# A fused FFT filter and mixture of experts: result tiles of 128 rows, earlier routing, fewer expert steps per filter piece, two result banks

## The chip, the cores and the metric

The kernel runs on one core of one Trainium2 chip. The metric is the device time of one execution in microseconds (us); the runs shown are the kernel before, three times: 1031.1, 1027.1 and 1033.96 us, median 1031.1.

The engines have the names of the profile: PE multiplies matrices (PEld is its weight load), DVE and ACT work on vectors, POOL here mostly issues DMAs with row indices, SP issues the other DMAs. Each engine works through its own queue in order.

## The reference

`x` is [8, 2496, 256]: 8 batches of 2496 tokens with 256 channels. Each batch is filtered along its tokens in the frequency domain, and each filtered token then goes through one of eight experts:

```
y      = irfft(rfft(x, axis=1) * (filt_r + 1j * filt_i), n=2496, axis=1)
logits = y @ w_gate + modality_bias[modality_id]        # [19968, 8]
e      = argmax(logits);  p = softmax(logits)[e]
out    = p * (relu(y @ w1[e]) @ w2[e])                  # w1 [8,256,1024], w2 [8,1024,256]
```

## The kernel before

**The filter** is a transform in two factors, 2496 = 48 x 52, with matrices that are made at the start. A batch goes through three stages, each in pieces of two columns; between the stages the data is turned by writing it to DRAM and reading it back in another order.
- Stage 1 (`stage1`, 13 pieces): two products with `w1m` (L363), ACT evicts them to `t1` (L366), SP writes `b1_d` (L369) after every second piece.
- Stage 2 (`stage2`, 12 pieces, the second half of a piece one step later): SP loads `t2` (L379); two products with `w2m` (L382); ACT evicts to `xf` (L394); DVE multiplies by the filter (L396, L397); four products with `a1m`, `a2m` (L389, L390); ACT evicts `z` (L403); SP writes `b2_d`.
- Stage 3 (`stage3`, 13 pieces, also one step apart): SP loads `t4`; two products with `wbm` (L433) give two result tiles of 96 tokens each; ACT and DVE in turn evict them to `yo` (L451, L453); four transposes (L441), DVE's copy `yT` (L443), four products with the gate weights (L446), and DVE adds them to the logits `lg` (L456). So a batch is 26 result tiles of 96 rows.

All these products, and the routing's, take their PSUM tiles from one pool of four banks, `fpsum`. The tile of the transposes holds the gate products as well.

**Routing.** `route` (DVE, one pair of small PE products with `psO`, L478 and the line behind it) finds each token's expert and its slot in `bins_d`, a DRAM table with a region for each expert. `table` (DVE) then makes the list of full blocks that a batch adds. `scatter` (L501, POOL, an indirect DMA) writes one result tile of 96 rows, token number and gate weight beside the data, to these slots; a batch has 26.

**The experts.** A block is 256 tokens of one expert; there are 85 (`KR` = 1, 10, 10, 10, 9, 10, 10, 25 by batch). SP loads it (`xs`, L575), five buffers. `turn` reads the expert's number into a register of PE (L584, `values_load`) and of DVE, copies the expert's first weights to `w1` (DVE, L588), copies the token numbers and gate weights to `meta` (DVE, L594, three buffers), transposes the block on PE (L598) and evicts it to `xT` (L599). Then follow four steps. Step q is `up` for the q-th quarter of this block's hidden units (four products, L609, then ACT's `hT`, L614) and `down` for the same quarter of the block before (four products, L622, which pick the second weights by PE's register). `turn` of the next block stands behind the second step. The result collects in one PSUM bank, `ops`, that opens with the first `down`; after the last, DVE evicts it in two halves times the gate weight to `osb` (L629, two buffers), and POOL writes each half to the rows of `out` that `meta` names (L632, an indirect DMA).

**The order** is that of the loops in the program; a scheduler keeps the order on each engine except where `behind(what, n)` puts an instruction behind a mark. Iteration `i` runs piece k = 0 to 13 of stage 1 for batch `i`, stage 2 for batch `i-1`, stage 3 for batch `i-2` and the scatters (two a piece) for batch `i-3`, then three expert steps (`STEPS`). After the pieces come `route` and `table` of batch `i-2`; blocks of batch `i-3` are opened for the experts then, at the end of its scatters. After iteration 11 the rest of the blocks run alone.

Of the kernel before, what the change touches and what calls it, by code (L numbers as in the profile page):

```python
# [28 lines left out]
def kernel(  # L29
# [32 lines left out]

    BLK = 256
# [48 lines left out]
    STEPS = 3  # L112
# [187 lines left out]
    keep = const_pool.tile([KA, E, NTT], F32)  # L300
# [40 lines left out]
    pp = ctx.enter_context(tc.tile_pool(name="fpsum", bufs=4, space=bass.MemoryType.PSUM))  # L341
# [7 lines left out]
    NP = NTT // EV  # L349
    st = [dict() for _ in range(B)]  # L350
# [57 lines left out]
    def stage3(g, k):  # L408

        t = k * EV  # L410
        if k == 0:
            yw = yp.tile([KA, NTT, RW], I32, tag="yo", name="yo")
            st[g]["yw"] = yw
            nc.gpsimd.iota(yw[:, :, DW:DW + 1], pattern=[[1, NTT], [1, 1]], base=g * S, channel_multiplier=NTT)
            mid_raw = sp.tile([KA, NTT, 2], I32, tag="midr")
            nc.sync.dma_start(mid_raw, mid32[g * S:(g + 1) * S].rearrange("(p t) two -> p t two", t=NTT))
            midf = sp.tile([KA, NTT], F32, tag="midf")
            nc.vector.tensor_copy(midf, mid_raw[:, :, 0])
            lg = sp.tile([KA, NTT, E], F32, tag="lg", bufs=2)
            st[g]["lg"] = lg  # L420
            nc.vector.tensor_mul(lg, midf[:, :, None].to_broadcast([KA, NTT, E]),
                                 biasd[:KA, None, :].to_broadcast([KA, NTT, E]))
            nc.vector.tensor_add(lg, lg, bias0[:KA, None, :].to_broadcast([KA, NTT, E]))
        yo = st[g]["yw"].bitcast(BF16)
        if k < NP:
            c, t0, t1 = chunk_of(t)
            if t == t0:
                src = b2_d[g].rearrange("s (jr t) c -> (s jr) t c", jr=4)
                st[g]["t4"] = bp.tile([KA, TCM, D], BF16, tag="t24", name="t4")
                nc.sync.dma_start(st[g]["t4"][:, 0:t1 - t0, :], src[:, t0:t1, :])  # L430
            ps = pp.tile([P, EV, D], F32, tag="ps")
            for i in range(EV):
                nc.tensor.matmul(ps[:KA, i, :], lhsT=wbm, rhs=st[g]["t4"][:, t - t0 + i, :], start=True, stop=True)  # L433
        if k > 0:
            tb = t - EV
# [317 lines left out]
```

## Time and profile before

| what | value |
|---|---|
| profiled execution, its time | 1031.97 us |
| its span in the profile | 1030.2 us |
| median of the three runs shown | 1031.1 us |
| mean granted clock of PE | 0.868 |
| busy, PE / DVE / POOL / ACT | 662.1 / 424.8 / 409.0 / 387.0 us |
| expert products, up / down | 222.2 / 227.6 us busy, 1360 each |
| scatters / output writes on POOL | 193.7 us for 208 / 166.8 us for 170 |
| routing products of the eight batches start at | 170.5, 244.5, 317.9, 416.7, 517.2, 612.8, 704.7, 796.3 us |

The times are of one execution, taken by the hardware profiler; all terms below are set against its 1031.97 us. A row of the groups reads: line, engine, operation, tiles, count, busy time, mean of one, idle time of the engine before them and what ended it. In a row of waits, "DVE meta L594 <- DMA out_dram" means that DVE's instruction of L594 had nothing to do until that DMA was seen to be done; the numbers are total, times and longest. In a row of the timeline the same stands in brackets behind the instruction. "remote" and "another core or an unknown queue" are waits whose releaser the profile does not know; this program has one core. "issue" is idle time without any wait. The granted clock reads 1.00 up to about 245 us of this trace, although products start 0.21 us apart there; from then on 0.50 and 1.00 take turns.

### The profile page before, as it was taken

The numbers are of one execution on the slowest core, as the hardware profiler recorded it, in microseconds if no ns is written. First come the engines' busy times: TensorE is split into PE (matmuls) and PEld (weight loads), VectorE is DVE, ScalarE is ACT, GpSimd is POOL, SyncE is SP. The second block draws the span as 40 slices with busy tenths as digits, with TensorE's granted clock in tenths as the row PEclk, the third lists the DMA queues.
The fourth block names the chain that finished last, engine by engine and source line by source line (L and its number), as shares of the span: only waits on it lengthen the run. The fifth ranks groups of instructions, "written<-read, shape, count | busy, mean of one in ns | idle before, by whom it ended". The sixth has DMA issues, their size and how long they took to land.

```text
span 1030.2 us, 16235 instructions
## 1 busy us (share of the span) xinstructions
PE 662.1 (64%) x4966; PEld 526.6 (51%) x4966; DVE 424.8 (41%) x1305; ACT 387.0 (38%) x697; POOL 409.0 (40%) x468
## 2 busy tenths in 40 slices
PE   0316377266645777687677776774777567768776
PEld 0205266255434666566565555563555445656554
DVE  8803145135325344633454463445335322333332
ACT  1115255143433455344444443441333233434333
POOL 6022201712442355435535543544355455333333
PEclk9999999999655898589979986896868787999999
DMA  9299965335436445534553344324111422212210
GB/s 146 36 207 208 219 147 127 91 91 129 108 87 140 115 120 116 129 99 126 123 146 92 96 120 111 91 62 113 58 57 54 118 68 78 73 62 67 68 42 2
DMA packets 95179, 106.66 MB, mean 104 GB/s; under 512 B 13226, under 2 KB 77520, under 8 KB 94994
## 3 DMA queue, kind: packets, MB, share of 16 engines
q0 software_dynamic: 32544, 52.04, 23.0%
q1 hardware_dynamic: 62554, 53.59, 20.1%
q8 instruction: 45, 0.74, 0.3%
q14 instruction: 36, 0.29, 0.1%
HBM read 74.27 MB, written 54.31 MB: 125 GB/s over the span
## 4 chain that ended last, share of the span: by engine, by line
PE 30%; issue 22%; DMA 13%; DVE 12%; another core or an unknown queue 10%; POOL 7%; ACT 4%; DVEq 1%; POOLq 0%; ACTq 0%; SPq 0%
PE hps L609 7%; PE ops L622 7%; DMA t<-b_d 5%; POOL out_dram L632 4%; DMA b_d<-t 4%; POOL bins_d L501 3%; DMA b_d<-z 2%; PE ps L433 2%; PE pz L389 2%; PE lt L446 2%; PE ps L363 2%; PE pz L390 2%; PE ps L382 2%; DVE osb L629 2%
## 5 line engine op out<-in xcount | busy, mean ns | idle before, releaser
L614 ACT ACTIVATE hT<-hps 128x512 f16<-128x512 f32 x340 | 197.0, 597 | 305.0 <-PE hps L609 164.3
L632 POOL DMA_INDIRECT out_dram<-osb,meta x170 | 166.8, 981 | 308.8 <-DVE osb L629 267.2
L622 PE MATMUL ops<-w2sb,hT 128*128 x1360 | 227.6, 291 | 46.8 <-DVE osb L629 46.3
L501 POOL DMA_INDIRECT bins_d<-yo,pos_i x208 | 193.7, 931 | 110.5 <-issue 69.7
L609 PE MATMUL hps<-xT,w 128*128 128x256 f16 x1360 | 222.2, 297 | 23.0 <-ACT hT L614 10.9
L622 PEld LDWEIGHTS <-hT 128*128 128x128 f16 x1360 | 140.6, 105 | 88.6 <-issue 57.7
L609 PEld LDWEIGHTS <-w 128*128 128x128 f16 x1360 | 138.9, 106 | 50.1 <-issue 18.2
L366 ACT CAST t<-ps 96x512 f16<-96x512 f32 x104 | 59.8, 583 | 127.7 <-PE ps L363 73.1
L599 DVE COPY xT<-pT 128x512 f16<-128x512 f16 x85 | 36.0, 424 | 146.4 <-PE pT L598 83.3
L403 ACT CAST z<-pz 104x512 f16<-104x512 f32 x96 | 56.7, 590 | 84.5 <-remote 30.7
L130 POOL DMA_DIRECT2D xt<-in_x_dram x32 | 18.2, 570 | 169.6 <-PE ps L363 158.8
L396 DVE TENSOR_TENSOR p<-xf,g 104x512 f16<-104x512 f16 x96 | 40.3, 420 | 109.1 <-ACT xf L394 94.4
L382 PE MATMUL ps<-t,w2m 104*104 104x256 f16 x192 | 52.8, 369 | 49.3 <-DMA t<-b_d 40.5
L389 PE MATMUL pz<-p,a1m 104*104 104x256 f16 x192 | 68.1, 364 | 21.0 <-issue 6.6
L433 PE MATMUL ps<-t,wbm 96*96 96x256 f16 x208 | 56.1, 354 | 37.4 <-DMA t<-b_d 15.2
L629 DVE TENSOR_SCALAR osb<-ops,meta 128x256 f32<-128x256 f32 x170 | 74.3, 476 | 9.3 <-PE ops L622 5.5
L363 PE MATMUL ps<-xt,w1m 96*96 96x256 f16 x208 | 59.0, 380 | 24.4 <-ACT z L403 8.5
L394 ACT CAST xf<-ps 104x512 f16<-104x512 f32 x96 | 56.3, 588 | 48.1 <-PE ps L382 34.2
L446 PEld LDWEIGHTS <-yT 128*96 128x96 f16 x416 | 40.9, 162 | 63.0 <-DVE yT L443 43.7
L446 PE MATMUL lt<-wg,yT 128*96 128x8 f16 x416 | 41.8, 207 | 47.2 <-DVE yT L443 32.7
L588 DVE COPY w<-w1sb 128x2048 f16 x85 | 58.8, 692 | 23.7 <-PE hps L609 18.1
L390 PE MATMUL pz<-xf,a2m 104*104 104x256 f16 x192 | 68.2, 365 | 0.0
(179 smaller groups left out, 687.3 us busy)
## 6 DMA issues: line engine op xcount, KB each, us to landing
xs<-bins_d SPq DMA_DIRECT2D x85, 130.0 KB
t<-b_d SPq DMA_DIRECT2D x24, 416.0 KB
b_d<-z SPq DMA_DIRECT2D x48, 208.0 KB
xt<-in_x_dram POOLq DMA_DIRECT2D x24, 384.0 KB
b_d<-t SPq DMA_DIRECT2D x48, 192.0 KB
t<-b_d SPq DMA_DIRECT2D x24, 384.0 KB
w1sb<-in_moe_w_dram POOLq DMA_DIRECT2D x8, 512.0 KB
w2sb<-in_moe_w_dram POOLq DMA_DIRECT2D x8, 512.0 KB
```

The source lines that it names most:

```text
L363: nc.tensor.matmul(ps[:KA, i, :], lhsT=w1m, rhs=xt[:, t - t0 + i, :], start=True, stop=True)
L382: nc.tensor.matmul(ps[:KB, i, :], lhsT=w2m[:, s + i, :], rhs=st[g]["t2"][:, s % SCH + i, :], start=True, stop=True)
L389: nc.tensor.matmul(pz[:KB, i, :], lhsT=a1m[:, s_ + i, :], rhs=p1[:, i, :], start=True, stop=False)
L390: nc.tensor.matmul(pz[:KB, i, :], lhsT=a2m[:, s_ + i, :], rhs=p2[:, i, :], start=False, stop=True)
L433: nc.tensor.matmul(ps[:KA, i, :], lhsT=wbm, rhs=st[g]["t4"][:, t - t0 + i, :], start=True, stop=True)
L446: nc.tensor.matmul(psL[:KA, i, :], lhsT=yT[:, i, dc, :], rhs=wg[:, dc, :], start=(dc == 0), stop=(dc == DC - 1))
L501: ins = nc.gpsimd.indirect_dma_start(out=bins_d[:, :], out_offset=IOA(ap=st[g]["pos"][:, t:t + 1], axis=0), in_=st[g]["yw"][:, t, :], in_o ...
L609: mm = nc.tensor.matmul(hps[:, k, :], lhsT=b["w1"][:, dc, ft * P:(ft + 1) * P], rhs=b["xT"][:, dc].rearrange("p i t -> p (i t)"), start=(d ...
L614: nc.scalar.activation(b["hT"][:, q * FQ:(q + 1) * FQ, :], hps, AF.Relu)
L622: nc.tensor.matmul(b["ops"][:, i, :], lhsT=b["hT"][:, ft, i * P:(i + 1) * P], rhs=w2sb[:, ds(b["ej"], 1), ft, :], start=(ft == 0 and i == ...
L629: nc.vector.tensor_scalar_mul(osb[:, i, :], b["ops"][:, i, :], gate[:, i, :])
L632: ins = nc.gpsimd.indirect_dma_start(out=out[:, :], out_offset=IOA(ap=b["meta"][:, i, 0:1], axis=0), in_=osb[:, i, :], in_offset=None, **kw)
```

## The change

The diff does six things.
1. **Result tiles of 128 rows.** 96 rows of one column and 32 rows of another column make one tile, so that 24 of the 26 columns become 18 full tiles, and the last two stay 96 rows: 20 tiles instead of 26. Each tile takes one more `wbm` product, of 32 output rows. Stage 3 has 10 pieces instead of 13, and a batch 20 scatters instead of 26. Token numbers come from a table `tok` by an addition instead of an iota in each batch; the modality numbers of all batches are loaded at the start (four DMAs, three of them in turn into one buffer) instead of one by one.
2. **Order.** `route` and `table` of a batch stand behind piece k = 11, its scatters begin with the next, two a piece through ten pieces, and its blocks are opened in the piece behind the last of them.
3. **Steps.** 2.25 instead of 3 expert steps per piece.
4. **Banks.** `fpsum` has three banks instead of four, `ops` two instead of one.
5. **Buffers.** `meta` has eight instead of three, `osb` three instead of two.
6. **Expert number.** PE's read of the next block's expert number (`which`) is taken out of `turn` and put behind the second `up` of the current block, ahead of that step's `down`.

```diff
-    STEPS = 3
+    STEPS = 2.25
-    mid32 = mid_h.ap().bitcast(I32).rearrange("(n two) -> n two", two=2)
+    mid32 = mid_h.ap().bitcast(I32).rearrange("(g p w) -> p g w", g=B, p=KA)
+    mids = const_pool.tile([P, B, NY], BF16)
...
+        nc.sync.dma_start(mraw[:KA], mid32)
...
+        for b in range(3):
+            nc.sync.dma_start(mraw[KA:P], mid32[b * KC:(b + 1) * KC])
+            nc.vector.tensor_copy(mids[KA:P, :, b:NYF:3], mv[KA:P, :, 3:4 * NYG:4, 0])
-    pp = ctx.enter_context(tc.tile_pool(name="fpsum", bufs=4, space=bass.MemoryType.PSUM))
+    pp = ctx.enter_context(tc.tile_pool(name="fpsum", bufs=3, space=bass.MemoryType.PSUM))
...
-            nc.gpsimd.iota(yw[:, :, DW:DW + 1], pattern=[[1, NTT], [1, 1]], base=g * S, channel_multiplier=NTT)
+            nc.gpsimd.tensor_single_scalar(yw[:, :, DW:DW + 1], tok, g * S, op=ALU.add)
...
-                nc.tensor.matmul(ps[:KA, i, :], lhsT=wbm, rhs=st[g]["t4"][:, t - t0 + i, :], start=True, stop=True)
+                a, b = divmod(u0 + i, 3)
+                t, tc_, c0 = (4 * a + b, 4 * a + 3, b * KC) if u0 < NYF else (4 * NYG + i, 4 * NYG + 1, 0)
+                nc.tensor.matmul(ps[:KA, i, :], lhsT=wbm, rhs=t4[:, t - t0, :], start=True, stop=True)
+                nc.tensor.matmul(ps[KA:P, i, :], lhsT=wbm[:, c0:c0 + KC], rhs=t4[:, tc_ - t0, :],
+                                 start=True, stop=True)
...
+    def which(b):
+
         with behind("up", 1):
             b["ej"] = nc.values_load(b["ej_i"], engines=(ET.PE,), min_val=0, max_val=E - 1)
+
+    def turn(b):
+
+        xh = b["xs"].bitcast(BF16)
...
-        b["meta"] = ep.tile([P, NI, 2], I32, tag="meta", bufs=3, name="meta")
+        b["meta"] = ep.tile([P, NI, 2], I32, tag="meta", bufs=8, name="meta")
...
-        if q == 0:
-            marks["up"].append(mm.ins)
+        marks["up"].append(mm.ins)
...
-            b["ops"] = op.tile([P, NI, D], F32, tag="ops", name="ops")
+            b["ops"] = op.tile([P, NI, D], F32, tag="ops", bufs=2, name="ops")
...
-            osb = ep.tile([P, NI, D], F32, tag="osb", bufs=2)
+            osb = ep.tile([P, NI, D], F32, tag="osb", bufs=3)
...
                 up(self.cur, self.q)
+                if self.q == 1:
+
+                    self.nxt = self.next()
             if self.prev is not None:
                 down(self.prev, self.q)
-            if self.q == 1 and self.cur is not None:
-                self.nxt = self.next()
+            if self.q == 1:
+                self.begin(self.nxt)
...
-            if 0 <= i - 3 < B and k < NP:
-                scatter(i - 3, k)
+            if to_bins:
+                g, n = to_bins[0]
+                if n < NPY:
+                    scatter(g, n)
+                    to_bins[0][1] += 1
+                else:
+                    if g == B - 1:
+                        pad_bins()
+                    moe.open(tabs[g], KR[g], g == B - 1)
+                    to_bins.pop(0)
+            if 0 <= i - 2 < B and k == NPY + 1:
+                route(i - 2)
+                tabs[i - 2] = table(KR[i - 2], i - 2 == B - 1)
+                to_bins.append([i - 2, 0])
...
-            for _ in range(STEPS):
+            owed += STEPS
+            while owed >= 1:
+                owed -= 1
                 moe.step()
```

The changed program's order of instructions shows where these edits land. Of PE's queue in the last blocks, before (L609 is up, L622 down, L584 the read of the expert number, L598 the transposes of the next block; the eight down products between the two steps are cut to one):

```order
L609 MATMUL hps<-xT,w_11804 128x256
L622 LDWEIGHTS hT
L622 ISA
L622 MATMUL ops<-w2sb,hT 128x256 [waits DVE_49]
...
L584 TENSOR_LOAD ej_i
L584 ISA x2
L598 LDWEIGHTS xs [waits DMAHW6_49]
L598 MATMUL pT<-ident,xs 128x128
...
L609 MATMUL hps<-xT,w_11804 128x256 [waits Activation_49]
```

and after (L645 is up, L657 down, L616 the read, L634 the transposes):

```order
L645 MATMUL hps<-xT,w_11436 128x256
L657 LDWEIGHTS hT
L657 ISA
L657 MATMUL ops<-w2sb,hT 128x256
...
L645 MATMUL hps<-xT,w_11436 128x256 [waits Activation_49]
...
L616 TENSOR_LOAD ej_i
L616 ISA x2
...
L634 LDWEIGHTS xs [waits DMAHW1_49]
L634 MATMUL pT<-ident,xs 128x128
```

The read of the expert number has moved from the place right ahead of the transposes, behind eight down products, to the place right behind an up group, with four down products between it and the transposes; and the first down product of a block no longer waits for DVE.

Of POOL's queue in an iteration of the middle, before (L632 is an output write, L501 a scatter, L130 a load of `x`):

```order
L632 DMA out_0_dram<-osb_4375,meta_4085 19968x256 x2
L501 DMA bins_d<-yo_2532,pos_i_3939 162048x130 x2
L632 DMA out_0_dram<-osb_4507,meta_4179 19968x256 x2
...
L632 DMA out_0_dram<-osb_4635,meta_4294 19968x256 x2
L501 DMA bins_d<-yo_2532,pos_i_3939 162048x130 x4
L130 DMA xt_4758<-in_x_dram 96x2048
```

and after (L667 the output write, L534 the scatter, L137 the load, L443 the token numbers):

```order
L667 DMA out_0_dram<-osb_5281,meta_4920 19968x256 x2
L534 DMA bins_d<-yo_4052,pos_i_5056 162048x130 x4
L667 DMA out_0_dram<-osb_5441,meta_5131 19968x256 x2
...
L534 DMA bins_d<-yo_4052,pos_i_5056 162048x130 x2
L443 TENSOR_SCALAR yo_6550<-tok_349 128x20
L667 DMA out_0_dram<-osb_6089,meta_5706 19968x256 x2
L667 DMA out_0_dram<-osb_6251,meta_5836 19968x256 x2
L667 DMA out_0_dram<-osb_6443,meta_6008 19968x256 x2
```

Before, two or four scatters stand between the writes of two blocks through the whole iteration; after, four stand between them in most of it, and at its end the writes of three or four blocks follow one another with no scatter between.

At the boundary of two iterations on PE, before (L478 is the routing product, L363, L382 and L433 the first products of the stages):

```order
L478 MATMUL psO_3928<-c_3926,Lexcl_65 96x8 [waits DVE_49]
L479 MATMUL psO_3928<-c_3926,ones_sq_70 128x8
...
L363 MATMUL ps_3981<-xt_3307,w1m_77 96x256 [waits DMASW4_49]
...
L382 MATMUL ps_3988<-t2_3986,w2m_79 104x256 [waits DMAHW4_49]
...
L433 MATMUL ps_4007<-t4_4005,wbm_78 96x256 [waits PE_49]
```

and after (L510 the routing product, L645 and L657 expert products, L392 and L418 stage 1 and the second half of stage 2):

```order
L510 MATMUL psO_3839<-c_3837,Lexcl_65 128x8 [waits DVE_49,Activation_49]
...
L645 MATMUL hps_3902<-xT_3659,w1_3657 128x256
...
L657 MATMUL ops_3744<-w2sb_375,hT_3486 128x256
...
L392 LDWEIGHTS w1m_77 [waits DMASW3_49]
L392 MATMUL ps_3917<-xt_3061,w1m_77 96x256
...
L418 MATMUL pz_3925<-p1_3820,a1m_80 104x256 [waits Activation_49]
```

The routing product stood alone ahead of the next iteration's first pieces; now it stands among the expert products of a piece, with the last pieces of the old iteration still behind it.

By the same orders, the up products of this many whole blocks stand ahead of the eight routing products: before 0, 0, 1, 11, 21, 31, 40 and 50, after 0, 1, 3, 11, 19, 27, 35 and 43.

More of the change, by code (lines that the diff above doesn't have):

```diff
@@ L60 @@
     KB = 2 * N2
+    KC = P - KA
+    assert KA == 3 * KC and NTT % 4 == 2
+    NYF = NTT // 4 * 3
+    NY = NYF + 2
+    NYG = NTT // 4
     BLK = 256
@@ L299 @@
     nc.vector.tensor_copy(jio, jio_i)
-    keep = const_pool.tile([KA, E, NTT], F32)
+    keep = const_pool.tile([P, E, NY], F32)
     nc.vector.memset(keep, 1.0)
@@ L477, in route @@
+        nc.vector.tensor_copy(c, sc[:, :, NY - 1])
         psO = pp.tile([P, 2, E], F32, tag="ps")
-        nc.tensor.matmul(psO[:KA, 0, :], lhsT=Lexcl[:KA, :KA], rhs=c, start=True, stop=True)
-        nc.tensor.matmul(psO[:, 1, :], lhsT=ones_sq[:KA, :], rhs=c, start=True, stop=True)
-        off = sp.tile([KA, E], F32, tag="off")
-        nc.vector.tensor_add(off, cnt[:KA], ecap[:KA])
-        nc.vector.tensor_add(off, off, psO[:KA, 0, :])
+        nc.tensor.matmul(psO[:, 0, :], lhsT=Lexcl, rhs=c, start=True, stop=True)
@@ L487, in route @@
         nc.vector.reduce_sum(pos, sc.rearrange("p e t -> p t e"), axis=AX.X)
[L488 removed]
+        pos_i = sp.tile([P, NY], I32, tag="posi", bufs=2)
         nc.vector.tensor_copy(pos_i, pos)
@@ L672, in next, with begin @@
             b = self.ready.pop(0)
-            turn(b)
-            self.fill()
-            return b
+            which(b)
+            return b
+        def begin(self, b):
+            if b is not None:
+                turn(b)
+                self.fill()
         def step(self):
```

106 lines of the change are left out of this document (59 added, 47 removed).

## The prediction

> **What bounds the kernel now.** I read the busy table by stage first, cut where the routing product (L478) of the third and of the last batch stands, then the waits, then the timeline. The columns of the table are window, length, busy time and instructions of PE, weight loads, DVE, ACT, POOL, then granted clock, DMA share, GB/s.
>
> ```profile
> span 1030.2 us, 16235 instructions
> L478 PE MATMUL psO<-c,Lexcl x16: 221/308/327, 170.5 to 796.5; 96*96 96x8 f32 x16
> 0.00:318.00 318.00, 150.04 (x903) 126.52 (x903) 131.70 (x394) 105.86 (x191) 93.11 (x131) 0.92 0.68 133
> 318.00:796.00 478.00, 348.71 (x2800) 277.36 (x2800) 216.71 (x709) 200.91 (x366) 221.26 (x239) 0.82 0.39 103
> 796.00:868.00 72.00, 42.69 (x317) 31.84 (x316) 22.39 (x72) 19.76 (x34) 39.77 (x42) 0.83 0.27 82
> 868.00:1023.00 155.00, 120.42 (x949) 90.92 (x948) 53.14 (x131) 60.47 (x106) 52.88 (x54) 0.93 0.19 58
> ```
>
> So there are three stages. In stage A (to 318 us) three filter batches run nearly alone. In stage B (318 to 796, five batches, 95.7 us each) filter pieces, scatters and expert blocks share PE; by the order of the instructions 1 block's up products are issued before B and 50 at its end, so B carries 49. Stage C (796 to the end, 234 us) holds the last 35 blocks: 10 beside the last 26 scatters, to about 868, then 25 alone in 155 us (two output writes each are most of POOL's 54 instructions there), 6.2 us a block. PE is busy 73% in B and 78% in the pure tail, and no other engine above 46%. What counts is therefore what PE waits for. In the pure tail:
>
> ```profile
> POOL out_dram L632 <- DVE osb L629: 90.6, 26, 5.2
> DVE meta L594 <- DMA out_dram<-osb,meta: 41.8, 25, 4.0
> PE ops L622 <- DVE osb L629: 23.4, 23, 2.8
> PEld L598 <- issue: 16.4, 23, 0.8
> ```
>
> and one block of it:
>
> ```profile
> 904.41 0.17 DVE L594 COPY meta<-xs 128x4 int32<-128x4 int32 x1 [3.15 <-DMA out_dram<-osb,meta]
> 904.54 0.69 DVE L588 COPY w<-w1sb 128x2048 f16 x1
> 905.15 0.87 DVE L629 TENSOR_SCALAR osb<-ops,meta 128x256 f32<-128x256 f32 x2
> 905.90 0.98 POOL L632 DMA_INDIRECT out_dram<-osb,meta  x1 [5.03 <-DVE osb L629]
> 906.07 1.87 PE L622 MATMUL ops<-w2sb,hT 128*128 x8 [2.66 <-DVE osb L629]
> 907.18 0.98 POOL L632 DMA_INDIRECT out_dram<-osb,meta  x1 [0.30 <-issue]
> 907.75 0.61 PE L598 MATMUL pT<-ident,xs 128*128 128x128 f16 x4
> 908.05 0.69 PEld L609 LDWEIGHTS <-w 128*128 128x128 f16 x4
> 909.52 0.43 PEld L609 LDWEIGHTS <-w 128*128 128x128 f16 x4
> 909.80 0.17 DVE L594 COPY meta<-xs 128x4 int32<-128x4 int32 x1 [0.97 <-DMA out_dram<-osb,meta]
> ```
>
> This is a ring. The meta copy (three buffers) waits until the output write of three blocks back has landed, which left POOL only just before; the weight copy and both osb evictions stand behind it on DVE; the single ops bank is freed by those evictions; PE's down products wait 2.66 us for them; and the next write leaves only then. 25 such waits make 1.7 us of DVE per block. Bare PE work of a block is 32 products at 0.108 (0.43 for four) plus four transposes (0.30, from 907.75 to the next weights at 908.05), **3.7 us**. The other 2.5 us of 6.2 are the ring and the 0.7 us behind each read of the expert number (16.4 us, 23 times).
>
> In B the same waits stand among others:
>
> ```profile
> DVE meta L594 <- DMA out_dram<-osb,meta: 41.5, 26, 2.5
> PE lt L446 <- DVE yT L443: 30.9, 17, 5.2
> PEld L598 <- issue: 20.1, 28, 1.4
> PE ops L622 <- DVE osb L629: 18.1, 20, 2.1
> ...
> PE lt L441 <- ACT t L366: 15.3, 8, 3.8
> ```
>
> The second row is filter work that waits for DVE, and part of what DVE was waiting for is the arrival of PE's signals during bursts of scatters. At 196 us the chain stands for 14.7 us while POOL issues nine scatters in a row, and what it waits for has no releaser that the profile knows:
>
> ```profile
> ## 4 chain that ended last, share of the span: by engine, by line
> PE 30%; issue 22%; DMA 13%; DVE 12%; another core or an unknown queue 10%; POOL 7%; ACT 4%; DVEq 1%; POOLq 0%; ACTq 0%; SPq 0%
> 196.06 14.73 another core or an unknown queue
> 196.12 0.92 POOL L501 DMA_INDIRECT bins_d<-yo,pos_i  x1 [0.30 <-issue]
> 197.35 0.92 POOL L501 DMA_INDIRECT bins_d<-yo,pos_i  x1 [0.30 <-issue]
> ...
> 205.92 0.92 POOL L501 DMA_INDIRECT bins_d<-yo,pos_i  x1 [0.31 <-issue]
> ```
>
> The unknown share, 10% of 1030 = 103 us, over 208 scatters is 0.5 us each; the worst place, 14.73 us over nine scatters, is 1.6 each. I take 0.5: it is the mean over all of them, and the burst at 196 is one of the few that nothing breaks. That the scatters are the cause is read from their place beside these waits, no more; if they are not, the price is 0.
>
> **The change part by part**, against the profiled execution (1031.97 us, 0.9 above the median 1031.1 of the runs).
>
> *Stage A: +4.* A result batch has 40 wbm products instead of 26, 40 transposes and 40 gate products instead of 52 each. The rows from 130.07 give their pace when the filter runs alone; the first row is for the start:
>
> ```profile
> PE tp L264 <- DVE w2m L228: 19.5, 1, 19.5
> 130.07 0.42 PE L390 MATMUL pz<-xf,a2m 104*104 104x256 f16 x1
> 130.28 0.64 PE L433 MATMUL ps<-t,wbm 96*96 96x256 f16 x2
> 130.71 0.53 PE L441 MATMUL lt<-ident,yo 96*128 96x96 f16 x4
> 131.04 0.63 PE L363 MATMUL ps<-xt,w1m 96*96 96x256 f16 x2
> ```
>
> One product per 0.21 us, four transposes in 0.33. So 14 × 0.21 − 24 × 0.08 = +1.0 a batch, +3 for three. That 32 columns cost as much as 96 is an assumption, with 0 as the other bound (a stream of 256 rows either way). In "TensorE: Matmul & The Clock Gate", section "Part 3: Packing small matmuls — row/col tiling", the Trainium skill says that products on disjoint tiles of the array run concurrently, about 4 ns apart; by it these 3 us would vanish, and no row here shows such a pair. The modality loads (eight, one a batch, are now four) move to the start, ahead of the first intermediate writes on SP's queue, and three of them reuse one buffer in turn, each after a DVE cast of the one before; behind these casts on DVE stands the scaling of the filter, for which the first second-stage products wait. No row shows such a chain. It costs between 0, hidden by the start's own wait (first of these rows), and three trips of a load (5.57 us, a row further down), +17; I take +3, nearer to the wait that is there already. Twelve fewer scatters: −6. Two more blocks are done in A (3 by the orders): 7.4 us of PE, half of it in PE's idle time, +4. Bounds −5 (no price for narrow products, the full one for scatters) to +15.
>
> *Stage B: 95.7 to 83.4 us per batch, −61.5 over five.* By the orders 3 blocks stand before it and 43 at its end, 40 instead of 49.
> - 1.8 fewer blocks per batch at 3.7: −6.7. They are not saved but go to C.
> - Two ops banks: 18.1 / 5 = −3.6. The down products start in the other bank while DVE evicts.
> - The expert number's read, moved behind the second group of up products, so that eight down products' worth of queued work covers it: of 20.1 / 5 = 4.0 I take −3. If PE's sequencer drains its queue there too, nothing.
> - Eight meta buffers: 41.5 / 5 = 8.3 us of DVE's waits go. Most of it reached PE through osb, counted above; −2 for yT and w behind it (0 to −8).
> - Six fewer scatters: −3 (by 1.6 it is −9.6, by the lower bound 0).
> - Filter products at the warm pace: 14 × 0.108 − 24 × 0.075, nothing. Evictions of 128 rows instead of 96 are as long (a piece is the same 512 columns) and three fewer; token numbers by an addition instead of an iota on POOL: nothing.
> - The order of the boundary: +4. Before, the routing product waits for DVE while the first pieces' loads run; now it is issued among expert products two pieces earlier, with DVE's routing and table behind it, and what is late next is the second stage, whose input has to be written and read back. The first row is the routing product's wait, the other two are such a trip:
>
> ```profile
> 317.94 0.46 PE L478 MATMUL psO<-c,Lexcl 96*96 96x8 f32 x2 [3.62 <-DVE c L476]
> 239.06 5.31 DMA b_d<-z
> 244.45 5.57 DMA t<-b_d
> ```
>
> Write and read are 10.9 us; PE has about 2.25 steps a piece over three pieces, some 6 us, to put in; 5 us of stall are left, against a routing wait of 3.6 that becomes covered. Taken +4 for the blocks that then come later; without that gain at the routing product 5.5, fully covered 0. The blocks of a batch are opened in the middle of the next iteration, 9 or 10 at a time, and 8 are used: experts are not starved.
>
> - Three filter banks instead of four: +2. The transposes wait today 15.3 us for a bank that ACT frees late (last row of B's waits), 3 a batch with four banks to turn; a piece takes five of them, and the one of transposes and gate products is held longest, over yT and the addition of lg. With three there are more such waits, by nothing at least, since the pieces come further apart than an eviction takes, and by all that B saves elsewhere at most (R3). I take two thirds of today's.
>
> Sum −12.3.
>
> In the same page, section "A second HAM failure mode: psum-queue depth-cycling", the Trainium skill speaks against this edit: cycling through PSUM banks lets PE idle shortly between groups and the clock swings between half and full. B's granted clock of 0.82 with four banks agrees that it swings. By that rule at half clock all through, 138 filter products a batch at 0.105 more are 14.5 us, 72 over five, and the total 1018, beyond R3.
>
> *Stage C: 234 to 206, −28.* Here 42 blocks are left instead of 35. About 5.6 stand beside the last 20 scatters: POOL needs 20 × 1.23 + 11 × 1.28 = 39 us (starts of scatters 1.23 apart, of writes 1.28, rows above), I take 42. The other 36.4 run alone: the meta wait has eight blocks of slack, the write's landing three osb buffers. The rows leave PE's 3.7 and some of the bubbles; between 3.9 and the 6.2 of today I take 4.3, near PE's own work because the ring's links are all cut: 156.5. The drain after the last products is as before, 7.2. Bounds by 3.9 and 6.2: −43 to +41.
>
> Sum: 1031.97 + 4 − 61.5 − 28 = **946 us**.
>
> **The rivals.**
> *R2, PE alone sets B.* If DVE's and the scatters' waits all hang on the same ring, B falls to PE's busy time: 348.7 / 5 − 6.7 = 63, plus 5.5 at the boundary, 68.5 a batch, −136; the tail at 3.9, −43. Time 857. For it: PE is the only engine above half. Against: busy time at a clock of 0.82 still has waits in it that other causes keep.
> *R3, the filter sets B.* Its chain from piece to piece (evict, multiply, transpose, evict yT, gate) on three banks and POOL's bursts keep the batch at 94 us, whatever the experts do; only C gains: 1032 + 4 − 8 − 28 = 1000. For it: PE's 30.9 us for yT. Against: with fewer steps per piece PE has less to do, and DVE fewer waits.
> *R4, the output writes set the pace.* If the next block still follows the landing of writes (osb now, instead of meta), the tail stays at 6.2 and B at 94: C is 42 + 225.7 + 7.2 = 275, +41, time 1069. It decides above 5.2 us per block, when the seven blocks moved to C cost more than B and C save. For it: POOL waits 90.6 us for osb. Against: three buffers allow the landing some 8 us.
> *No change*, the meta wait or bubbles being hidden behind something equal: about 1031.
>
> **How the numbers follow.** Forecast 0.57, R2 0.17, R3 0.16, R4 0.06, no change 0.04. Faster by over 1% (about what a measurement of this kernel can tell): 0.57 + 0.17 + 0.16 = 0.90; within 1%: 0.04; slower: 0.06. The range goes from 866, a little above R2, to 1002, past R3; the forecast's own, by the bounds of B's parts and 3.9 to 5.0 per block in C, is 895 to 988.
>
> **What would show it.** Right: no meta wait on out_dram in the tail; blocks 4 to 4.6 us apart there; PE waiting for osb under 5 us in all; routing products about 83 us apart in B. Wrong: batches of B over 90 us with PE waiting for yT or for banks, or a clock below 0.8 there (R3); blocks over 5.2 us apart with osb waiting for writes (R4); batches under 72 (R2). If the time is right but B and C miss in opposite directions, the working was wrong.

## The result, and the profile after

The changed kernel takes 934.74 us (median of 4, 928.01 to 937.54), the kernel before, run beside it, 1029.1 us. The ratio is **0.9075**, with a 95% interval of 0.9002 to 0.9147. The profiled execution took 937.54 us, 94.4 less than the one of before. The forecast was 946 with a range of 866 to 1002.

The routing products first, then the busy table, cut at the third and the eighth of them and at the last scatter (columns as in the prediction):

```profile
span 935.8 us, 15940 instructions
L510 PE MATMUL psO<-c,Lexcl x16: 247/256/361, 171.3 to 723.1; 128*128 128x8 f32 x16
0.00:310.00 310.00, 168.09 (x924) 117.41 (x924) 130.51 (x385) 107.68 (x194) 85.92 (x121) 0.91 0.69 136
310.00:723.00 413.00, 312.93 (x2432) 230.23 (x2432) 191.27 (x631) 180.68 (x328) 183.98 (x194) 0.84 0.43 114
723.00:772.00 49.00, 24.04 (x190) 18.60 (x191) 14.85 (x53) 11.36 (x20) 29.42 (x30) 0.79 0.29 92
772.00:924.00 152.00, 144.78 (x1303) 121.55 (x1302) 71.80 (x179) 82.95 (x146) 70.43 (x72) 0.99 0.28 86
```

| stage | before | forecast | measured |
|---|---|---|---|
| A, to the third routing product | 317.9 | +4 | 310.0, -7.9 |
| B, to the eighth | 478.4 | -61.5 | 412.9, -65.5 |
| C, to the end | 233.9 | -28 | 212.8, -21.1 |

A's minus is mostly bookkeeping: the routing product now stands two pieces earlier in its iteration. The first product of the second stage behind it comes at 323.0 instead of 321.7. The pure tail is the clearest gain: PE is busy 145 of 152 us, and 36 blocks take 4.2 us each. Before it was 5.9: the prediction's 6.2 shares 155 us among 25 blocks, but the 949 products of that stretch, at 36 a block, are 26.4 blocks.

The waits of the tail (total, times, longest) answer to the four rows of before:

```profile
POOL out_dram L667 <- DVE osb L664: 70.5, 35, 3.7
...
DVE meta L630 <- DMA out_dram<-osb,meta: 8.5, 9, 2.1
...
PEld L634 <- issue: 0.2, 1, 0.2
```

The meta copy's 41.8 us are 8.5, PE's wait for osb (23.4) has no row any more, and what is left of the idle time ahead of the transposes (16.4 before) is 0.2. One block of it in the timeline:

```profile
803.21 0.35 PEld L657 LDWEIGHTS <-hT 128*128 128x128 f16 x3 [0.35 <-issue]
803.24 0.96 POOL L667 DMA_INDIRECT out_dram<-osb,meta  x1 [1.90 <-DVE osb L664]
803.27 0.17 DVE L630 COPY meta<-xs 128x4 int32<-128x4 int32 x1
...
804.51 0.97 POOL L667 DMA_INDIRECT out_dram<-osb,meta  x1 [0.30 <-issue]
...
807.37 0.55 PEld L657 LDWEIGHTS <-hT 128*128 128x128 f16 x4 [0.25 <-issue]
807.41 0.97 POOL L667 DMA_INDIRECT out_dram<-osb,meta  x1 [1.92 <-DVE osb L664]
```

The meta copy at 803.27 goes beside the output write that has just begun at 803.24, instead of behind its landing; the next block's write follows 4.2 us later.

In B the rows that carried terms of the sum read now:

```profile
ACT hT L649 <- remote: 41.0, 9, 8.0
...
PE ps L462 <- ACT t L395: 17.9, 8, 4.1
...
PEld L477 <- DVE yT L474: 10.1, 15, 2.5
...
PE lt L477 <- DVE yT L474: 6.1, 8, 2.2
```

PE's wait for yT fell from 30.9 to 6.1 us; the wait for a filter bank that ACT frees has moved from the transposes to the first product of stage 3 and is about as large (17.9 after 15.3). What grew is ACT's wait without a known releaser ahead of `hT`, from 20.5 us in seven pieces to 41.0 in nine, although all such waits of the run together fell from 214 us to 138. They still stand beside the bursts of scatters. So do those where C misses its 7 us:

```profile
762.98 0.60 PE L657 MATMUL ops<-w2sb,hT 128*128 x4
...
768.01 0.91 POOL L534 DMA_INDIRECT bins_d<-yo,pos_i  x1 [0.30 <-issue]
770.39 0.42 DVE L635 COPY xT<-pT 128x512 f16<-128x512 f16 x1 [7.57 <-remote]
...
771.17 1.08 ACT L649 ACTIVATE hT<-hps 128x512 f16<-128x512 f32 x2 [8.68 <-remote]
...
771.82 1.01 PE L645 MATMUL hps<-xT,w 128*128 128x256 f16 x4 [8.24 <-ACT hT L649]
```

PE had ended its products at 763.6; ACT and DVE go on only when the last four scatters are through. C so takes 48.9 us up to 771.8, where 42 were forecast. From there to the last product at 928.7 it takes 156.9 us and then 7.1 more, as forecast (156.5 and 7.2).

### The profile page after: what moved, and what is told of

The parts are those of the page before. It is cut to its first block, busy times and chain, and to the rows that moved or that the text cites. A ratio compares the mean times of both kernels' runs of the same rounds, so it can differ in the third digit from the quotient of the medians.

```text
span 935.8 us, 15940 instructions
## 1 busy us (share of the span) xinstructions
PE 654.5 (70%) x4886; PEld 491.7 (53%) x4886; DVE 410.6 (44%) x1249; ACT 385.0 (41%) x689; POOL 375.6 (40%) x423
## 4 chain that ended last, share of the span: by engine, by line
PE 55%; DMA 10%; issue 10%; another core or an unknown queue 9%; DVE 9%; ACT 6%; POOL 0%; DVEq 0%; POOLq 0%; SPq 0%; ACTq 0%
PE hps L645 16%; PE ops L657 16%; DMA b_d<-t 5%; PE ps L463 4%; PE ps L462 4%; PE lt L472 3%; DMA t<-b_d 3%; ACT t L395 3%; PE pz L418 3%; PE pz L419 2%; PE ps L392 2%; PE pT L634 2%; PE ps L411 2%; ACT hT L649 2%
## 5 line engine op out<-in xcount | busy, mean ns | idle before, releaser
L667 POOL DMA_INDIRECT out_dram<-osb,meta x170 | 167.7, 987 | 272.8 <-DVE osb L664 223.5
L645 PE MATMUL hps<-xT,w 128*128 128x256 f16 x1360 | 232.5, 291 | 32.8 <-issue 17.9
L657 PE MATMUL ops<-w2sb,hT 128*128 x1360 | 228.4, 288 | 10.8 <-issue 9.6
L534 POOL DMA_INDIRECT bins_d<-yo,pos_i x160 | 156.7, 979 | 50.9 <-issue 48.6
L645 PEld LDWEIGHTS <-w 128*128 128x128 f16 x1360 | 131.1, 103 | 62.4 <-issue 40.0
L657 PEld LDWEIGHTS <-hT 128*128 128x128 f16 x1360 | 138.6, 103 | 45.2 <-issue 19.1
L411 PE MATMUL ps<-t,w2m 104*104 104x256 f16 x192 | 49.0, 348 | 78.4 <-DMA t<-b_d 54.3
L137 POOL DMA_DIRECT2D xt<-in_x_dram x32 | 17.6, 549 | 214.6 <-PE ps L392 175.7
L462 PE MATMUL ps<-t,wbm 96*96 96x256 f16 x160 | 58.7, 367 | 36.0 <-ACT t L395 17.9
L418 PE MATMUL pz<-p,a1m 104*104 104x256 f16 x192 | 61.3, 334 | 23.4 <-DVE p L425 7.0
L411 PEld LDWEIGHTS <-w2m 104*104 104x104 f16 x192 | 29.6, 164 | 83.5 <-DMA t<-b_d 55.6
L392 PE MATMUL ps<-xt,w1m 96*96 96x256 f16 x208 | 53.5, 356 | 16.2 <-ACT t L395 15.9
L419 PE MATMUL pz<-xf,a2m 104*104 104x256 f16 x192 | 62.5, 340 | 0.3
L474 DVE COPY yT<-lt 128x512 f16<-128x512 f16 x80 | 33.7, 421 | 62.4 <-PE lt L472 45.8
```

Source lines behind the costliest of these rows:

```text
L392: nc.tensor.matmul(ps[:KA, i, :], lhsT=w1m, rhs=xt[:, t - t0 + i, :], start=True, stop=True)
L411: nc.tensor.matmul(ps[:KB, i, :], lhsT=w2m[:, s + i, :], rhs=st[g]["t2"][:, s % SCH + i, :], start=True, stop=True)
L418: nc.tensor.matmul(pz[:KB, i, :], lhsT=a1m[:, s_ + i, :], rhs=p1[:, i, :], start=True, stop=False)
L419: nc.tensor.matmul(pz[:KB, i, :], lhsT=a2m[:, s_ + i, :], rhs=p2[:, i, :], start=False, stop=True)
L462: nc.tensor.matmul(ps[:KA, i, :], lhsT=wbm, rhs=t4[:, t - t0, :], start=True, stop=True)
L534: ins = nc.gpsimd.indirect_dma_start(out=bins_d[:, :], out_offset=IOA(ap=st[g]["pos"][:rows, t:t + 1], axis=0), in_=st[g]["yw"][:rows, t, ...
```

## The experiments

All experiments ran on other chips of the same kind. There the kernel before takes 898 to 901 us in every call, not 1029, so each kernel is compared with the runs of the kernel before beside it. The column of us is the ratio times 898.5. The stages are cut at the third and the eighth routing product of each trace; "pace" is the mean distance of two blocks' first up products once the last scatter is through, without the first such distance. Stages and pace come from one execution each, which lies up to 11 us from the column of us (904 us with three meta buffers), so differences of a few us between stages say little.

| kernel | ratio to before | interval | us, ratio times 898.5 | A | B | C | pace |
|---|---|---|---|---|---|---|---|
| before | 1 |  | 898 | 268 | 405 | 221 | 5.7 |
| changed | 0.919 | 0.915 to 0.923 | 825 | 293 | 340 | 188 | 3.8 |
| changed, 3 meta buffers | 0.994 | 0.989 to 0.999 | 893 | 295 | 353 | 255 | 5.6 |
| changed, 1 ops bank | 0.972 | 0.969 to 0.976 | 874 | 291 | 335 | 236 | 5.0 |
| changed, 1 ops and 4 filter banks | 0.953 | 0.949 to 0.958 | 856 | 286 | 336 | 236 | 5.0 |
| changed, late read | 0.917 | 0.910 to 0.924 | 824 | 291 | 333 | 188 | 3.7 |
| changed, 3 steps | 0.918 | 0.913 to 0.923 | 825 | 299 | 371 | 157 | 3.8 |
| changed, scatters spaced | 0.987 | 0.984 to 0.990 | 887 | 285 | 395 | 203 | 3.8 |
| changed, meta copy held, 4 buffers | 0.889 | 0.885 to 0.893 | 798 | 292 | 321 | 191 | 3.8 |
| before, 6 meta buffers | 0.965 | 0.959 to 0.970 | 867 | 269 | 377 | 220 | 5.6 |
| before, all but tiles and order | 0.971 | 0.966 to 0.975 | 872 | 276 | 333 | 260 | 5.5 |
| the same, meta copy held | 0.880 | 0.875 to 0.885 | 791 | 275 | 318 | 199 | 3.7 |

**The two kernels on these chips.** No edit.

> The changed kernel itself, on the chips of the experiments, where the kernel before takes 898 us instead of 1029 and the traces so far show no wait without a known releaser. If the early read of the expert number is worth what my sum says (+15 in B, +24 in the tail when undone), it is 35 to 40 us faster than the run with the late read (0.917 of before): 0.873 to 0.88, 785 to 790 us. Rival, the read only shifts a wait: within 1% of that run, 0.908 to 0.926, 815 to 832 us. Its ratio on the first chip was 0.9075.

> The kernel before itself, for its trace on these chips. If the 10% of unknown waits in the chain of the first trace are PE's signals that scatters delay, they are gone here and nearly all of the 131 us are missing in A and B, while the 25 blocks of the tail still take 6.2 us each. Rival, the whole program runs faster here: the tail's blocks are shorter in the same proportion, about 5.4 us.

The ratio of the changed kernel, 0.919, is near the one of the result, and within 1% of the run with the late read (0.917), as the rival had it; the time is not that of the first chip. The trace of before shows where the time differs:

```profile
0.00:268.00 268.00, 145.57 (x902) 125.12 (x902) 130.22 (x392) 105.12 (x191) 91.76 (x128) 0.87 0.78 157
268.00:673.00 405.00, 324.27 (x2801) 260.93 (x2801) 215.83 (x714) 201.71 (x366) 228.66 (x243) 0.88 0.46 122
673.00:737.00 64.00, 40.63 (x324) 31.04 (x325) 23.11 (x73) 21.72 (x38) 40.04 (x42) 0.87 0.31 93
737.00:885.00 148.00, 114.60 (x928) 87.44 (x928) 51.83 (x129) 58.18 (x102) 51.46 (x53) 0.95 0.20 61
```

A is 50 us shorter and B 74, the stretch behind the last scatters only 7 (148 us instead of 155), and not one wait is put down to an unknown releaser, where the first trace has 214 us of them on all engines together. PE keeps going under the same scatters (rows of PE and POOL alone):

```profile
178.59 0.42 PE L389 MATMUL pz<-p,a1m 104*104 104x256 f16 x1
178.68 1.00 POOL L501 DMA_INDIRECT bins_d<-yo,pos_i  x1 [13.16 <-DVE off L481]
178.81 0.42 PE L390 MATMUL pz<-xf,a2m 104*104 104x256 f16 x1
...
179.99 1.01 POOL L501 DMA_INDIRECT bins_d<-yo,pos_i  x1 [0.30 <-issue]
...
180.20 0.63 PE L363 MATMUL ps<-xt,w1m 96*96 96x256 f16 x2
...
181.31 0.92 POOL L501 DMA_INDIRECT bins_d<-yo,pos_i  x1 [0.30 <-issue]
181.47 0.42 PE L389 MATMUL pz<-p,a1m 104*104 104x256 f16 x1
```

So what was expected of the unknown waits came, A and B being 123 of the 136 us between the two profiled executions, and the rival fell. That these waits by themselves cost the 123 us was not isolated, and why the first chip has them was not found: no experiment ran on it.

**Three meta buffers.**

```diff
-        b["meta"] = ep.tile([P, NI, 2], I32, tag="meta", bufs=8, name="meta")
+        b["meta"] = ep.tile([P, NI, 2], I32, tag="meta", bufs=3, name="meta")
```

> The changed kernel with three meta buffers again. If the ring over meta is what set the tail's pace, the meta copy waits for the landing of a recent output write again, DVE's queue stands behind it, and the tail goes from 4.2 to 5.0 to 5.8 us per block (37 blocks, +30 to +55 us), B a few us more: 970 to 995 us. Rival, the second ops bank alone cut the ring and the meta wait is idle time of DVE that nobody waits for: within 5 us of the changed kernel's 935.

The whole gain is gone but 0.6%: 68 us more by the ratios, nearly all of it in C, at 5.6 us a block. The ring theory held and was too small. The waits of its tail:

```profile
DVE meta L630 <- DMA out_dram<-osb,meta: 131.2, 35, 7.3
...
PE hps L645 <- DVE xT L635: 47.4, 28, 3.8
```

3.7 us a block, and PE waits behind it for xT although it has two ops banks.

**One ops bank,** with three filter banks and with four.

```diff
-            b["ops"] = op.tile([P, NI, D], F32, tag="ops", bufs=2, name="ops")
+            b["ops"] = op.tile([P, NI, D], F32, tag="ops", name="ops")
```

> The changed kernel with one ops bank (the other banks as they are, one bank left empty). My sum has 3.6 us a batch in B and, by the 23.4 us over 23 blocks of before, about 1 us a block in the tail for PE's wait for osb: +18 and +37, together 975 to 995 us. Rival, with eight meta buffers DVE evicts at once, so that one bank is enough: under +12 us, below 947.

> The changed kernel with the banks as before: one for ops, four for the filter. Against the run with one ops bank and three filter banks it shows what the fourth filter bank is worth: 2 us a batch by my sum, 10 to 16 us in all. Rival R3 (the filter's banks set B): 30 us or more, B's batches below 75 us.

48 us more with one bank (55 forecast), but all of it in C, 5.0 us a block; B is as short as with two. The two waits that PE has in the tail of this run, and not in that of the changed kernel on these chips:

```profile
PE ops L657 <- issue: 18.8, 35, 0.7
PE ops L657 <- DVE osb L664: 12.6, 35, 3.8
```

The fourth filter bank is then worth 17 us by the ratios, about what the sum had; the two profiled executions differ by 5, all in A, so that the place of the rest is not shown.

**The late read.**

```diff
-        marks["up"].append(mm.ins)
+        if q == 0:
+            marks["up"].append(mm.ins)
...
             b = self.ready.pop(0)
-            which(b)
             return b
 
         def begin(self, b):
             if b is not None:
+                which(b)
                 turn(b)
```

> The changed kernel with PE's read of the expert number where it was, behind the down products and right ahead of the transposes. By my sum +3 us a batch in B and 0.6 to 0.7 us a block in the tail: +15 and +24, 970 to 978 us. Rival, the read's 0.7 us only shifts a wait that PE has anyway: within 8 us of 935.

No difference: 0.917 against 0.919. In its tail the transposes follow the down products without a gap, although by the edit the read stands between them:

```profile
748.35 0.60 PE L658 MATMUL ops<-w2sb,hT 128*128 x4
...
748.68 0.32 PEld L634 LDWEIGHTS <-xs 128*128 128x128 f16 x4
748.79 0.39 PE L634 MATMUL pT<-ident,xs 128*128 128x128 f16 x4
748.96 0.37 PEld L645 LDWEIGHTS <-w 128*128 128x128 f16 x4
```

So the gap of before belonged to the ring. In the kernel before with six meta buffers, where the ring stays closed and the read is late (below), the idle time ahead of the transposes is still 16.9 us in 23 pieces of the tail. Why the gap comes with the ring is not shown; likely PE then has no other work queued.

**Three steps a piece.**

```diff
-    STEPS = 2.25
+    STEPS = 3
```

> The changed kernel with 3 steps a piece. By the order 52 blocks instead of 43 stand ahead of the last routing product. My sum prices a block at 3.7 us in B and 4.3 in the tail, so moving nine of them gains some 5 us: 925 to 935 us. Rival, experts run out of opened blocks in B with 3 steps, as long idle stretches without up products in the trace of before (20 to 27 us in each iteration) suggest: the time is 950 to 975, and such stretches come back.

Same time: A 6 and B 30 us longer, C 32 shorter, with nine more blocks ahead of the last routing product. That is 3.5 us a block either way: blocks are moved, as the sum had it. Stretches of 8 to 15 us without an up product are there in each iteration, where the changed kernel has only two over 8 us in B and C, so the rival's mechanism is present, but it cost nothing that shows.

**Six meta buffers in the kernel before,** and **all but tiles and order.** (The second edit is the diff of the change without the tiles, the order, the third osb buffer, and with six meta buffers.)

```diff
-        b["meta"] = ep.tile([P, NI, 2], I32, tag="meta", bufs=3, name="meta")
+        b["meta"] = ep.tile([P, NI, 2], I32, tag="meta", bufs=6, name="meta")
```

> The kernel before with six meta buffers instead of three and nothing else (eight do not fit into its memory). If the ring over meta sets the tail, the tail goes from 6.2 to about 5 us a block (25 blocks, -30 us) and B gains up to 2 us a batch: 990 to 1000 us. Rival, one ops bank keeps the ring closed: within 8 us of 1029.

> The kernel before with all of the change but the tiles and the order: 2.25 steps, two ops banks, three filter banks, six meta buffers, the expert number read early; 26 tiles of 96 rows, routing and opening at the end of an iteration, two osb buffers. My sum gives the tiles and the order +4 in A, and in B -3 for scatters and +4 for the boundary a batch: nearly nothing. So 935 to 955 us. Rival, what shortens B is the order (blocks opened in the middle of an iteration, a shorter scatter phase): B stays at 90 us a batch or more and the time is 985 to 1010.

Both expectations failed in the tail. Twice as many buffers left it at 5.6 and 5.5 us a block. The first kernel's 0.965 does lie where it was expected (990 to 1000 of 1029 us is 0.962 to 0.972), but by luck: the gain is in B. The second's 0.971 lies in its rival's range (985 to 1010 us), and not for the rival's reason, since B is short. In this second kernel, with two ops banks, the meta copy still waits for the landing of writes:

```profile
DVE meta L597 <- DMA out_dram<-osb,meta: 117.4, 32, 5.2
...
PE hps L612 <- DVE xT L602: 49.2, 31, 3.2
```

The order of the built programs tells why: the scheduler moves the meta copy ahead as far as it has buffers and loaded blocks. In the tail, at the meta copy of block 74, these blocks are evicted and this one's write is waited for:

| kernel | blocks evicted by then | the copy waits for the write of block | writes of slack |
|---|---|---|---|
| before, 3 buffers | 0 to 71 | 71 | 0 |
| before, 6 buffers | 0 to 68 | 68 | 0 |
| changed, 3 buffers | 0 to 71 | 71 | 0 |
| changed, 8 buffers | 0 to 67 | 66 | 1 |
| changed, 4 buffers, copy held (next run) | 0 to 71 | 70 | 1 |

With three and with six the copy waits for the write that has just been issued. Eight are more than the loads let it run ahead, and one write of slack is left. B shortened all the same, by 27 us in the first and by 72 in the second, which has 40 blocks there instead of 49.

**The meta copy held in place.** This tests that reading. In the changed kernel with four buffers:

```diff
-        b["meta"] = ep.tile([P, NI, 2], I32, tag="meta", bufs=8, name="meta")
-        nc.vector.tensor_copy(b["meta"], b["xs"][:, :, DW:DW + 2])
+        b["meta"] = ep.tile([P, NI, 2], I32, tag="meta", bufs=4, name="meta")
+        with behind("w1", 1):
+            nc.vector.tensor_copy(b["meta"], b["xs"][:, :, DW:DW + 2])
```

and the same `with` line, with six buffers, in the kernel with all but tiles and order.

> The changed kernel with four meta buffers instead of eight, and the meta copy held behind the weight copy of its own block, so that it isn't moved ahead of its place. By the built order the copy then waits for the write before the last one issued, as with eight buffers that run ahead; with three, and with six in the kernel before, it waits for the last one. If that slack of one write is what opens the ring, the time is that of the changed kernel: 0.91 to 0.925 of before, 817 to 832 us, a tail of 3.8 us a block. Rival, the number of buffers is what counts: near the run with three, 0.98 or more and 5.2 to 5.6 us a block.

> The run with all of the change but the tiles and the order, its meta copy held in place as well (one line; six meta and two osb buffers stay). If the copy's wait for the last write was all that kept its tail at 5.5 us a block, 36 blocks fall to 3.8 (-62 us) and the stretches before stay: 805 to 815 us, 0.895 to 0.905, faster than the changed kernel's 0.919, so that the tiles and the order cost time. Rival 1, two osb buffers keep the ring closed: 0.95 or more, tail at 5 or above. Rival 2, the tiles and the order are worth nothing either way: 0.915 to 0.925.

Four held buffers have the tail of eight, 3.8 us a block: it was the slack, not the number. And 27 us more are gained than with eight, which no theory had (0.91 or more was expected), by the traces 20 of them in B. There the copy that ran ahead waited for something else, the load of its block; over the whole run of the changed kernel on these chips

```profile
DVE meta L630 <- DMA xs<-bins_d: 66.0, 27, 7.9
...
DVE meta L630 <- DMA out_dram<-osb,meta: 12.6, 13, 2.1
```

and with the copy held

```profile
DVE meta L631 <- DMA out_dram<-osb,meta: 26.8, 16, 6.2
...
DVE meta L631 <- DMA xs<-bins_d: 3.6, 1, 3.6
```

That these waits are what B gained is likely, but was not tested by itself.

The second kernel falls from 0.971 to 0.880 by that one `with` line, 81 us: C by 61 as expected, B by 15, which was expected to stay. It is the fastest here, 4% below the changed kernel, and it has tiles of 96 rows, the old order and two osb buffers.

**Scatters spaced.**

```diff
             tc.add_to_no_dep_group("bins", ins.ins)
+            with behind("out", 1):
+                nc.gpsimd.iota(idle, pattern=[[1, 1024]], base=0, channel_multiplier=0)
```

> The changed kernel with an instruction of about 1 us on POOL (numbers written to an unused tile) behind each scatter, so that no two scatters follow one another directly; it computes the same. If back-to-back scatters delay PE's signals, they come at half the rate and the waits without a known releaser shrink: -10 to -30 us, 905 to 925. Rival 1, any work of POOL delays the signals or the output writes behind it: +20 us or more. Rival 2, POOL's time is off the path: within 5 us of 935.

61 us slower, 54 of them in B: rival 1. Since no wait on these chips lacks a known releaser, it says nothing on delayed signals. Of 167 us more of POOL's busy time a third is paid, and behind each added instruction stand scatters and output writes. But what was paid for is not shown to be POOL's queue: the added instruction also makes DVE slower. With the same 1249 instructions DVE is busy 442 us instead of 410, and its copies take longer; here is the meta copy (behind the first bar: us in all, mean ns) in the changed kernel and in this run:

```profile
L630 DVE COPY meta<-xs 128x4 int32<-128x4 int32 x85 | 15.0, 180 | 82.9 <-DMA xs<-bins_d 66.0 <-DMA out_dram<-osb,meta 12.6 <-DVE lg L487 1.7
...
L632 DVE COPY meta<-xs 128x4 int32<-128x4 int32 x85 | 41.9, 493 | 119.0 <-DMA xs<-bins_d 97.1 <-DMA out_dram<-osb,meta 18.9 <-DVE lg L487 0.9
```

The run can't tell the two apart.

## Why the prediction was right, and where its working was not

By most of its own signs the prediction was right: blocks 4.2 us apart in the tail, no wait of PE for osb there, routing products 82.6 us apart in B, and of the meta wait a rest of 8.5 us. By its last sign the working was wrong, for B and C miss in opposite directions: B is 4.0 us below its forecast and C 6.9 above.

**The tail's ring** was right as the cause, and on the chips of the experiments it is nearly the whole gain: without the meta buffers 0.994, without the second ops bank 0.972. Two statements of it failed. The copy did not wait "until the output write of three blocks back has landed", but for the last write issued, since it runs ahead; and eight buffers are not "eight blocks of slack" but one. Held in place, four do the same.

**A sum of separate terms** was the wrong form for it. The meta copy and the ops bank are links of one ring: either alone puts the tail at 5.0 to 5.6 us a block, so each undone costs 48 to 68 us of the same 73. The sum gave B -3.6 for the bank and -2 for meta a batch; on the other chips the bank is worth nothing in B, the meta buffers 12 us over five batches. B's 64 us there are 30 for the blocks that 2.25 steps move away, and 27 come with more meta buffers in the kernel before (only those 12 when they are taken from the changed one, so these do not add up either); the other parts, undone one by one, change B by 7 at most.

**Stage C, -28:** measured -21.1. The block's price was 4.3 and came out as 4.2. The 42 us beside the scatters became 48.9: 46.0 to the end of the last scatter and 2.9 more until PE goes on, at the end of a stall of 8.2 us (763.6 to 771.8) that the sum had not. The 6.2 of before was 5.9, as counted above. That leaves the 4.3 as it is, but the tail of the rival R4 would be 215 us instead of 225.7.

**The read of the expert number, -3 a batch and part of the tail's 0.6,** failed: 0.917 without it. The step "of 20.1 / 5 = 4.0 I take -3" took a symptom of the ring for a cost.

**Filter banks, +2 a batch:** the size is near the run with four banks (17 us by the ratios, 10 in the sum for B), the place was not shown.

**Fewer blocks in B and more in C:** right; moving nine blocks back by 3 steps leaves the time as it was.

**Tiles and order, +4 in A, about +1 a batch in B by scatters and boundary:** with the copy held in both kernels, theirs is 0.889 and without them 0.880. A loses 17 us, B 3, C gains 8; with them two more blocks are done in A and two fewer in C, so that some 7 us of A's loss come back in C. So on these chips the tiles and the order cost about 1%, and A's term was mis-sized (+17 for +4).

One piece of that can be read from the traces. The sum priced the 14 more `wbm` products of a batch at 0.21 us each in A, 2.9 in all, and at 0.108 in B, 1.5, ahead of what fewer transposes save. The rows come from the two runs with the copy held, first new tiles in the changed kernel, then a pair of old ones, both where the granted clock is 1.00:

```profile
318.53 0.27 PE L462 MATMUL ps<-t,wbm 96*96 96x256 f16 x1
318.73 0.28 PE L463 MATMUL ps<-t,wbm 96*32 96x256 f16 x1
318.94 0.31 PE L462 MATMUL ps<-t,wbm 96*96 96x256 f16 x1
319.18 0.28 PE L463 MATMUL ps<-t,wbm 96*32 96x256 f16 x1
...
318.69 0.38 PE L433 MATMUL ps<-t,wbm 96*96 96x256 f16 x2
```

The product of 32 columns starts 0.20 to 0.24 us behind that of 96, and the next one again as much; the two of 96 start 0.11 apart. So they do not run at once, and going from one to the other costs more than two equal products. Summed in these two runs from the start of each `wbm` product to that of the next product of any kind, the three batches of A take 39.8 us with the new tiles and 16.2 with the old, the five of B 47.1 and 18.7: 7.9 and 5.7 us a batch more.

The third osb buffer and the meta buffers differ between the two kernels as well, so that this 1% is not theirs alone to the last us.

**The price of a scatter, 0.5 us,** belongs to the first chip. The experiments' chips have no wait without a known releaser at all; on the first one fewer scatters may well have gained what A lost elsewhere (A there is +1.3 by the second stage's first product, +25 by the routing product here). That was not tried, since no run was on it. The unknown waits did fall with the scatters, from 10% of a chain of 1030 us to 9% of 936; at one price per scatter they would have fallen from 103 to 79 us, and 84 is what the page gives:

```profile
PE 55%; DMA 10%; issue 10%; another core or an unknown queue 9%; DVE 9%; ACT 6%; POOL 0%; DVEq 0%; POOLq 0%; SPq 0%; ACTq 0%
```

**The clock.** The rule of the Trainium skill ("TensorE: Matmul & The Clock Gate", "A second HAM failure mode: psum-queue depth-cycling"), weighed against the three filter banks, did not decide: B's granted clock is 0.84 with three banks, 0.82 with four before, and PE's clock is 0.99 in the tail. In the two runs with one ops bank, which differ in the fourth filter bank alone, B's clock is 0.94 with three and 0.93 with four.

That the total came within 12 us of the forecast owes something to errors of both signs: the terms for the read and for the bank in B have nothing behind them in these runs, and yet B fell by more than forecast. Which edits gave B its 65 us on the first chip was not taken apart there. The forecast's own range, 895 to 988, was narrower than the bounds that the prediction lists: all of them at one end give about 830, at the other about 1030.

## What to carry to other kernels

When a wait for a buffer's release is in a ring, look in the built order where the waiting instruction really stands: a scheduler that hoists a cheap copy can spend the added buffers on running ahead, and the copy still waits for the newest release. Three more buffers did nothing for the tail here, five more left one write of slack. Hold the copy behind its own block's work, and few buffers do. And don't add up the links of a ring as separate gains; take one out at a time and read the stage where the ring turns.

## What the runs showed of the hardware that was not expected

The same program, with the same data, took 1029 us on one chip and 898 to 901 on three others, with equal durations of scatters (916 and 913 ns, median). Of 136 us between two profiled executions all but some 7 are in the stages with scatters. On the slow chip ACT and DVE stand up to 14.7 us (8.7 in the changed kernel) without a known releaser while POOL issues indirect DMAs in a row, in the example above after PE has ended its products; on the others they never do. The changed kernel's tail is slower there too, without scatters, 4.2 us a block instead of 3.8. The cause is open.

Two more: a product of 32 columns behind one of 96 costs twice the start distance of two products of 96 (0.20 to 0.24 against 0.11 us), and an instruction of POOL that writes a tile made DVE's copies slower (180 to 493 ns for the meta copy, 706 to 887 for the weight copy, mean).
